# w_phi loads on SyncE's queue, a phi mask in three parts, and new orders on five engines, in a transformer layer tuned by explicit instruction lists

## Chip, cores, metric

One core of a Trainium2 chip. The metric is the device time of one execution in microseconds (us). Ratios are those of the record, of one kernel's fast runs to the other's of the same rounds, with a 95% interval; they are not quite the ratio of the medians that are quoted.

## The reference, cut

```python
x = A_x                                     # 1 x 2048 x 576, bf16
h = x + A(layernorm(x))                     # linear attention, 32 heads of 18
h2 = h + B(layernorm(h))                    # B normalizes again; 576 -> 4608 gelu -> 576
# A: q, k, v = x @ wqkv;  pq = q @ w_phi[head];  pk = k @ w_phi[head]
#    phi = [softmax(p), softmax(-p)];  kv = phi_k^T v;  z = sum phi_k
#    o = (phi_q kv) / (phi_q z + 1e-6);  return o @ wo
```

The kernel folds w_phi into the k and q weights first (it transposes wk, multiplies it with a block-diagonal phi), then walks over 16 tiles of 128 tokens.

## The kernel before

Every instruction is recorded under a label, and PLAN lists for each engine the order of the labels. Semaphore waits are derived from what each instruction reads and writes. So a label that stands early in an engine's list, and waits, holds up everything behind it on that engine. The labels that matter (t is a tile, c a block of 128 of the 576 features):

- lx, lwk, lwv, lphi: loads of x, k weights, v weights, w_phi. wq: transposing loads of q weights. B: bulk loads of MLP and output weights. T: transpose of a normalized tile by DMA (tiles 0 and 1: by TensorE).
- S: statistics of a tile, P: its rstd (the reciprocal of its standard deviation) on GpSimd, Y: its normalization. STAT and NORM say which engine does S and Y (D VectorE, A ScalarE, P GpSimd).
- A: transposes of wk and copies out of PSUM, the memory that TensorE writes to. F: folded k weights. W: folded q weights. K, V, G, Q: the products per tile for keys, values, kv and queries. R, M: VectorE's sums and scalings of a tile.

```python
STAT = "DDDADDAADADADADA"
NORM = "DDDPPPPPPPPPAPPP"
PHI = "pool"
PLAN = {
    "pe": (
        "warm0 warm2 warm3 A0 A1 warm4 A2 A3 A4 T0 F0 F1 F2 F3 F4 T1 K0 W0 W2 W3 W1 K1 V0 W4 K2 W5 V1 K3 G0 "
        # ... cut: K, V, G, Q of later tiles, attention of tiles 0 and 1
    "dve": (
        "z0 zy3 zy2 pads z2 z4 zy1 S0 z3 z1 zy0 S1 A1 Y0 Y1 A5 S2 F1 F5 F3 pads2 Y2 S4 S5 R0 M0 R1 W5 M1 R2 "
        # ... cut
    "pool": (
        "- P0 phi P1 masks P2 P3 Y3 P4 Y4 Y5 P6 Y6 Y7 P8 Y8 Y9 P10 Y10 Y11 b1c P12 P14 Y15 Y13 Y14 Ns1 L0 L1"
    "sp": (
        "lwk0 lx1 lx2 lwk2 lwk4 lwv4 lx3 wq3 wq2 wq0 wq4 wq1 lwv T2 B16 T3 B3 T4 b1 x4 B11 T5 x5 T6 T7 T8 B8 "
        "B1 B17 T9 B5 B0 T10 T11 B2 T12 B13 B12 B9 T13 T14 T15 B10 w2b0 B15 B7 B6 w2b8 B4 B14"
# ... cut
    P.at("phi")                       # one operation, waits for all three w_phi loads
    P.add(PHI, lambda e: e.tensor_tensor(
        phib[0:126, :, :].rearrange("p b (g j) -> p b g j", g=7),
        wphi_st[0:126, :, :].unsqueeze(2).to_broadcast([126, 5, 7, DH]),
        mask7[0:126, :, 0:1].unsqueeze(1).to_broadcast([126, 5, 7, DH]), ALU.mult),
        reads=WPH + [res("mask7")], writes=[res("phib")])
```

The softmax here doesn't subtract the row's maximum and nothing guards it: scores larger than these inputs give would overflow.

Of the kernel before, what the change touches and what calls it, by code (L numbers as in the profile page):

```python
# [6 lines left out]
ALU = mybir.AluOpType  # L7
# [231 lines left out]
def bass_sequential_preLN__linear_kernel_hedgehog__mixer_channel_mlp__prompt_kernel(  # L239
# [12 lines left out]
    _build(nc, A_x, A_wqkv, A_w_phi, A_wo, B_w1, B_b1, B_w2, B_b2, out)  # L252


PAIRS = [(0,), (1,), (2,), (3,)] + [(t, t + 1) for t in range(4, 16, 2)]
STAT = "DDDADDAADADADADA"
NORM = "DDDPPPPPPPPPAPPP"
TURN = "EEDDDDDDDDDDDDDD"
TCOPY = "AADD"
ACOPY = "ADAAAD"  # L260
WARM = "0111"
FCOPY = "ADADAD"
WCOPY = "AAAAAD"
PHI = "pool"
PLAN = {
    "pe": (
        "warm0 warm2 warm3 A0 A1 warm4 A2 A3 A4 T0 F0 F1 F2 F3 F4 T1 K0 W0 W2 W3 W1 K1 V0 W4 K2 W5 V1 K3 G0 "
        "Q0 V2 G1 K4 V3 G2 K5 Q1 G3 V4 Q2 K6 G4 V5 Q3 K7 V6 Q4 K8 G5 V7 G6 K9 G7 Q5 V8 K10 Q6 G8 V9 K11 Q7 "
        "V10 K12 G9 Q8 V11 G10 K13 G11 V12 K14 Q9 V13 G12 K15 Q10 V14 G13 V15 Q18 Q11 G14 G15 Q19 N0 N1 Q20 "
        "Q12 Q13 Q14 O0 Q15 L0 O1 Q16 L1 Q17 Q21 U0 Q22 U1 Q23"  # L270
    ).split(),
    "act": (
        "lx0 lphi2 lphi0 lphi1 exp A0 S3 A2 A4 A3 T0 F0 F2 F4 T1 K0 W0 W1 K1 S6 K2 W2 W3 W4 K3 S7 Q0 K4 S9 K5 "
        "Q1 S11 Q2 K6 Q3 K7 S13 Q4 K8 K9 Q5 S15 K10 Y12 Q6 K11 Q7 K12 Q8 K13 K14 Q9 K15 Q10 Q11 Q18 Q19 Q20 "
        "Q12 Q13 Q14 O0 Q15 O1 Q16 Q17 Q21 U0 Q22 Q23 gelu"
    ).split(),
    "dve": (
        "z0 zy3 zy2 pads z2 z4 zy1 S0 z3 z1 zy0 S1 A1 Y0 Y1 A5 S2 F1 F5 F3 pads2 Y2 S4 S5 R0 M0 R1 W5 M1 R2 "
        "M2 R3 M3 R4 S8 M4 R5 M5 R6 S10 M6 R7 M7 R8 S12 M8 S14 R9 M9 R10 M10 R11 M11 R12 M12 R13 M13 R14 R15 "
        "M14 M15 kvr Nc0 Ns0 Nc1 Ni0 Nm0 Ni1 Nm1 L0 L1 U1"  # L280
    ).split(),
    "pool": (
        "- P0 phi P1 masks P2 P3 Y3 P4 Y4 Y5 P6 Y6 Y7 P8 Y8 Y9 P10 Y10 Y11 b1c P12 P14 Y15 Y13 Y14 Ns1 L0 L1"
    ).split(),
    "sp": (
        "lwk0 lx1 lx2 lwk2 lwk4 lwv4 lx3 wq3 wq2 wq0 wq4 wq1 lwv T2 B16 T3 B3 T4 b1 x4 B11 T5 x5 T6 T7 T8 B8 "
        "B1 B17 T9 B5 B0 T10 T11 B2 T12 B13 B12 B9 T13 T14 T15 B10 w2b0 B15 B7 B6 w2b8 B4 B14"
    ).split(),
}

# [1 line left out]
def _build(nc, A_x, A_wqkv, A_w_phi, A_wo, B_w1, B_b1, B_w2, B_b2, out):  # L292
    S = 2048
    D = 576
    H = 32
    DH = 18
# [13 lines left out]
    P = Prog(nc)  # L310
# [34 lines left out]
    wkst = w2a[:, 0:6, :].rearrange("p m d -> p (m d)")[:, 0:3200].rearrange("p (c k) -> p c k", c=5)  # L345
    w2b = RB[:, 0:NW2B * D].rearrange("p (m d) -> p m d", m=NW2B)

    mask7 = sb("mask7", [128, 7, 19])
# [4 lines left out]
    mask25 = OTR[:, 0:475].rearrange("p (h d) -> p h d", h=25)  # L353
    wphi_st = OTR[:, 480:570].rearrange("p (b j) -> p b j", b=5)
    phib = OTR[:, 576:1206].rearrange("p (b j) -> p b j", b=5)
    oT = [OTR[:, 640 * i:640 * i + 640].rearrange("p (c t) -> p c t", c=5) for i in range(2)]
    bns = sb("bns", [128, 12], F32)
    kvr = sb("kvr", [128, 2, H, 20])
# [20 lines left out]
    bank = [Bank() for _ in range(8)]  # L379
# [3 lines left out]
    def res(name):  # L383
        if name not in R:
            R[name] = Res(name)
        return R[name]

    def rr(fmt, n):
# [7 lines left out]
          reads=[res("ident")], writes=[res("ident")])  # L396
# [3 lines left out]
          reads=[res("maskf")], writes=[res("maskf")])  # L400
    P.add("pool", lambda e: e.affine_select(maskf[:, :, :], maskf[:, :, :], pattern=[[18, 7], [0, 19]],
                                            compare_op=ALU.is_ge, fill=0.0, base=17, channel_multiplier=-1),
          reads=[res("maskf")], writes=[res("maskf")])
    P.add("pool", lambda e: e.tensor_copy(mask7[:, :, :], maskf[:, :, :]),
          reads=[res("maskf"), res("tmpo")], writes=[res("mask7")])

    WPH = rr("wphi{}", 3)
# [3 lines left out]
    P.add("dve", lambda e: e.memset(wkst[64:128, 4, :], 0.0), writes=[res("wkst4b")])  # L411
    P.add("dve", lambda e: e.memset(wkst[:, 0:4, D:D + 2], 0.0), writes=[res("wkstpad")])
    P.add("dve", lambda e: e.memset(wkst[0:64, 4, D:D + 2], 0.0), writes=[res("wkstpad")])
    P.at("z2")
    P.add("dve", lambda e: e.memset(wphi_st[:, 3, :], 0.0), writes=[res("wphi1")])
    P.at("z3")
    P.add("dve", lambda e: e.memset(wkT[:, :, 576:640], 0.0), writes=[res("wkTpad")])
    for i in range(NYB):
# [13 lines left out]
    def load(q, dst, src, writes, reads=()):  # L432
        ch = P.chan(f"ld{nch[0]}", q)
        nch[0] += 1
        P.dma(ch, lambda e: e.dma_start(dst, src), reads=reads, writes=writes)
# [15 lines left out]
    for n, (dst, src, w) in enumerate((  # L451
            (wphi_st[0:126, 0:3, :], A_w_phi[0:21].rearrange("(b h) i j -> (h i) b j", b=3), "wphi0"),
            (wphi_st[0:72, 3, :], A_w_phi[21:25].rearrange("h i j -> (h i) j"), "wphi1"),
            (wphi_st[0:126, 4, :], A_w_phi[25:32].rearrange("h i j -> (h i) j"), "wphi2"))):
        P.at(f"lphi{n}")
        load("act", dst, src, [res(w)])
    P.at("exp")
    P.add("act", lambda e: e.activation(st2[:, 0, 0:1], neghalf[:, 0:1], AF.Exp), reads=[res("neghalf")],
          writes=[res("s2_0"), res("table")])
    for c in (0, 2):  # L460
        P.at(f"lwk{c}")
        load("sp", wkst[:, c:c + 2, 0:D], A_wqkv[128 * c:128 * c + 256, D:2 * D].rearrange("(c p) m -> p c m", p=128),
             [res(f"wkst{c}"), res(f"wkst{c + 1}")])
    P.at("lwk4")
    load("sp", wkst[0:64, 4, 0:D], A_wqkv[512:576, D:2 * D], [res("wkst4")])
    P.at("lx1")
# [32 lines left out]
    def ln1_rstd(ts):  # L499
        P.at(f"P{ts[0]}")  # L500
        t0, n = ts[0], len(ts)
        st = lambda k: st1[:, k, t0:t0 + n]
        sq = [t for t in ts if STAT[t] == "A"]
        if sq:
# [10 lines left out]
        for t in ts:  # L515
            if NORM[t] == "A":
                P.add("pool", lambda e, t=t: e.tensor_scalar(st1[:, 3, t:t + 1], st1[:, 6, t:t + 1], st1[:, 5, t:t + 1],
# [59 lines left out]
    def stats(t):  # L577
        (ln1_stats_act if STAT[t] == "A" else ln1_stats_dve)(t)
        for g in PAIRS:
            if t == g[-1]:  # L580
                ln1_rstd(g)

    def lnorm(t):
        if NORM[t] != "A":
            ln1_norm({"D": "dve", "P": "pool"}[NORM[t]], t)
            return
# [7 lines left out]
    def turn_y(t):  # L594
        if TURN[t] == "E":
            ln1_petr(t, 512 * 6, {"A": "act", "D": "dve"}[TCOPY[t]])
        else:
# [20 lines left out]
    for c in range(5):  # L618
        P.at(f"A{c}")
        if c < 4:  # L620
            for b in range(5):
                turn_mm(c, b, 512 * c + 128 * b if b < 4 else 2048 + 128 * c)
            ps_copy(ACOPY[c], wkT[0:126, 0:4, 128 * c:128 * c + 128],
                    ps_all[0:126, 512 * c:512 * c + 512].rearrange("p (b k) -> p b k", b=4),
                    [bank[c]], [res(f"wkT{c}")])
            P.at(f"warm{c + 1}")
            warm(int(WARM[c]))
        else:
            for b in range(5):
                turn_mm(c, b, 2560 + 64 * b)  # L630
            ps_copy(ACOPY[4], wkT[0:126, :, 512:576], ps_all[0:126, 2560:2880].rearrange("p (b k) -> p b k", b=5),
                    [bank[5]], [res("wkT4")])
    P.at("A5")
    ps_copy(ACOPY[5], wkT[0:126, 4, 0:512], ps_all[0:126, 2048:2560], [bank[4]], [res("wkTb")])
    turn_y(0)

    P.at("phi")
    P.add(PHI, lambda e: e.tensor_tensor(
        phib[0:126, :, :].rearrange("p b (g j) -> p b g j", g=7),
        wphi_st[0:126, :, :].unsqueeze(2).to_broadcast([126, 5, 7, DH]),  # L640
        mask7[0:126, :, 0:1].unsqueeze(1).to_broadcast([126, 5, 7, DH]), ALU.mult),
        reads=WPH + [res("mask7")], writes=[res("phib")])
    stats(1)
    P.at("pads")
    P.add("dve", lambda e: e.memset(wv[64:128, 4, :], 0.0), writes=[res("wvpad")])
# [7 lines left out]
    for g in range(4):  # L653
        n = 7 if g < 3 else 4
        P.add("pool", lambda e, g=g, n=n: e.tensor_copy(mask25[:, 7 * g:7 * g + n, :], mask7[:, 0:n, :]),
              reads=[res("mask7")], writes=[res("mask25")])
    P.add("pool", lambda e: e.tensor_copy(
        kvr[:, :, 0:25, 19:20], mask25[:, :, 0:1].unsqueeze(1).to_broadcast([128, 2, 25, 1])),
        reads=[res("mask25")], writes=[res("kvr1")])
    P.add("pool", lambda e: e.tensor_copy(  # L660
        kvr[:, :, 25:32, 19:20], mask7[:, :, 0:1].unsqueeze(1).to_broadcast([128, 2, 7, 1])),
        reads=[res("mask7")], writes=[res("kvr1")])

    def weff_mm(wT, reads, c, b, lo, hi, col):
        gs = DH * HG[b][1]
        P.add("pe", lambda e: e.matmul(ps_all[:, col:col + hi - lo], wT[0:gs, b, 128 * c:128 * c + 128],  # L666
                                       phib[0:gs, b, lo:hi], start=True, stop=True),
              reads=reads + [res("phib")], banks=[bank[col // 512]])

    def weff_main(wT, reads, c, bk):  # L670
        for b in range(4):
# [6 lines left out]
    for c in range(5):  # L678
# [3 lines left out]
        weff_tail(wkT, rd, c, 5)  # L682
        ps_copy(FCOPY[c], weffk[:, c, 0:512], ps_all[:, 512 * c:512 * c + 512], [bank[c]], [res(f"weffk{c}")])
    P.at("F5")
    ps_copy(FCOPY[5], weffk[:, :, 512:576], ps_all[:, 2560:2880].rearrange("p (c f) -> p c f", c=5),
            [bank[5]], [res("weffkb")])
# [122 lines left out]
    def weffq_units():  # L809
# [8 lines left out]
        for c in range(5):  # L818
            weff_tail(wqT, rd, c, 5)
        ps_copy(WCOPY[5], weffq[:, :, 512:576], ps_all[:, 2560:2880].rearrange("p (c f) -> p c f", c=5),  # L820
                [bank[5]], [res("weffqb")])
# [110 lines left out]
    def attn_oT(t, bset=None):  # L932
        P.at(f"O{t}")
        ob = t % 2
        rd = [res(f"obuf{ob}"), res(f"opad{ob}")]
        wr = [res(f"oT{ob}")] + (WPH + [res("phib"), res("mask25")] if t < 2 else [])
        if bset is None:
            dma_tr(oT[ob], obuf[ob][:, :], rd, wr)
        else:
            pe_tr(obuf[ob], oT[ob], 512 * bset[2], rd, wr, dup=True)  # L940
# [101 lines left out]
    while bulk:  # L1042
# [6 lines left out]
        reads=[res("mask25")], writes=[res("kvra")], banks=[bank[5], bank[6]])  # L1049
# [3 lines left out]
        reads=[res("mask7")], writes=[res("kvrb")], banks=[bank[7]])  # L1053
# [4 lines left out]
    for m0 in range(0, NW2B, 8):  # L1058
# [5 lines left out]
    S1, S2 = (6, 7, 5), (1, 2, 0)  # L1064
# [24 lines left out]
          reads=[res("neghalf")] + rr("Eq{}", NR), writes=[res("sums0")])  # L1089
# [118 lines left out]
    for r in range(NR):  # L1208
        a, b = RT * (r + 1), RT * (r + 1) + 1
# [49 lines left out]
```

## Time and profile before

| | us |
|---|---|
| time, median of the first 3 runs | 412.71 (412.15 to 413.18) |
| span of the profiled execution | 409.6 |
| first phi-weight product (F0) starts | 11.17 |
| first MLP product starts | 96.5 |
| from there to the end | 313.05 |

The page of the kernel before: busy time per engine, then TensorE's granted clock (the share of the full clock that its throttle lets through) in tenths over 40 slices of 10.2 us.

```profile
span 409.6 us, 11671 instructions
...
PE 398.2 (97%) x5001; PEld 289.3 (71%) x5001; DVE 180.4 (44%) x451; ACT 180.6 (44%) x418; POOL 97.7 (24%) x130
...
PEclk9899999999999999999999999999999999999999
```

TensorE is the limit, and in the MLP, three quarters of the span, it hardly waits. The change leaves that part's code alone. So all that can be had is in the first 96.5 us. The chain of waits of the kernel before, 5 to 17 us (start, us, what), shows the prologue:

```profile
2.33 3.73 DMA OTR<-in_A_w_phi_dram
6.06 1.72 issue
7.78 1.30 POOL OTR L638
9.08 0.20 POOL st L511
...
9.35 0.58 POOL st L513
...
10.04 0.43 DVE ybuf L526
10.47 0.61 DVE RA L604
...
11.17 1.50 PE ps_all L666 x30
12.67 0.42 PE ps_all L563 x5
13.09 2.42 PE ps_all L744 x10
```

L638 is the phi mask, L511 and L513 tile 1's rstd, L526 its normalization, L604 the copy A5, L666 the F products, L744 a K group. The 1.72 us called issue are GpSimd's wait for the last of the three w_phi loads, which landed at 7.65 us. The rstd stands behind the mask in GpSimd's list although it does not need it. K0 takes 2.42 us, at half clock, later K groups 1.23 us. TensorE's waits in the first 100 us (us in total, times, longest):

```profile
PE ps_all L666 <- DVE RA L604: 2.6, 1, 2.6
PE ps_all L744 <- DMA yT<-ybuf: 1.4, 2, 1.1
...
```

The second line is the K groups waiting for a tile transposed by DMA (yT).

### The profile page before, as it was taken

Reading aid. Unit: us, or ns where it says so; the run is one execution under the profiler, and the core shown is the slowest. Engines: PE = TensorE matmul, PEld = TensorE weight load, DVE = VectorE, ACT = ScalarE, POOL = GpSimd, SP = SyncE. Lnnn points to the kernel's source line nnn. Section 1 sums busy time; section 2 is a strip of 40 time slices with the busy share of each in tenths; the row PEclk is TensorE's granted clock in tenths of the full one; section 3 lists DMA queues with packets and bytes.
Section 4 is the critical chain, followed back from the end, with each engine's and each line's share of the span. In section 5 each row is a group of like instructions: output and inputs, shape, how many; then the busy total and the mean of one; then the engine's idle time right before and its main releaser. Section 6 shows DMA issues by size and latency. Waiting matters only on the chain.

```text
span 409.6 us, 11671 instructions
## 1 busy us (share of the span) xinstructions
PE 398.2 (97%) x5001; PEld 289.3 (71%) x5001; DVE 180.4 (44%) x451; ACT 180.6 (44%) x418; POOL 97.7 (24%) x130
## 2 busy tenths in 40 slices
PE   5999999999999999999999999999999999999996
PEld 2566666858965796589559956985697579658953
DVE  4898998886445125422443234234324412300000
ACT  5686764568850274037205710660075026404700
POOL 4868680012202202210320022002200220111000
PEclk9899999999999999999999999999999999999999
DMA  9875974292211100111120111111100110000000
GB/s 231 187 173 103 256 190 99 67 387 99 35 25 41 32 18 18 32 33 20 27 30 23 19 34 30 29 24 32 32 18 19 30 32 19 18 14 19 2 2 29
DMA packets 45596, 25.87 MB, mean 63 GB/s; under 512 B 32745, under 2 KB 44521, under 8 KB 45545
## 3 DMA queue, kind: packets, MB, share of 16 engines
q1 hardware_dynamic: 44784, 24.97, 24.8%
q8 instruction: 39, 0.64, 0.6%
q10 hardware_dynamic: 760, 0.17, 0.3%
q14 instruction: 13, 0.10, 0.1%
HBM read 15.13 MB, written 2.36 MB: 43 GB/s over the span
## 4 chain that ended last, share of the span: by engine, by line
PE 87%; DVE 5%; DMA 3%; POOL 2%; issue 1%; ACT 1%; ACTq 0%; DVEq 0%; POOLq 0%
PE ps_all L1125 35%; PE ps_all L1193 35%; PE ps_all L950 5%; PE ps_all L744 4%; PE ps_all L761 3%; PE ps_all L829 2%; DMA yT<-ybuf 2%; PE ps_all L850 2%; PE ps_all L799 1%; POOL ybuf L526 1%; DMA OTR<-in_A_w_phi_dram 1%; DVE x_all L970 1%; ACT RB L751 1%; PE ps_all L666 0%; DVE RB L784 0%
## 5 line engine op out<-in xcount | busy, mean ns | idle before, releaser
L1136 ACT ACTIVATE RA<-ps_all,b1T 128x256 bf16<-128x256 f32 x288 | 115.0, 479 | 176.7 <-PE ps_all L1125 162.1
L1125 PE MATMUL ps_all<-yT,w1sb 64*128 64x256 bf16 x2304 | 151.9, 269 | 0.0
L1125 PEld LDWEIGHTS ps_all<-yT,w1sb 64*128 64x128 bf16 x2304 | 136.2, 94 | 5.1
L1193 PE MATMUL ps_all<-w2a,RA 128*128 128x512 bf16 (+1 forms) x640 | 96.2, 286 | 0.0
L1193 PEld LDWEIGHTS ps_all<-w2a,RA 128*128 128x128 bf16 x640 | 45.8, 98 | 35.6 <-ACT RA L1136 1.5
L1125 PE MATMUL ps_all<-yT,w1t 64*128 64x256 bf16 x288 | 70.8, 270 | 0.0
L1193 PE MATMUL ps_all<-RB,RA 128*128 128x64 bf16 (+1 forms) x512 | 67.7, 286 | 0.0
L1202 DVE TENSOR_TENSOR WQ<-ps_all,tmpo 128x64 bf16<-128x64 f32 (+1 forms) x32 | 14.7, 458 | 101.2 <-PE ps_all L1193 88.9
L1193 PEld LDWEIGHTS ps_all<-RB,RA 128*128 128x128 bf16 x512 | 33.5, 98 | 32.3
L970 DVE SCALAR_TENSOR_TENSOR x_all<-ps_all,x_all 128x576 bf16<-128x576 f32 x16 | 12.1, 758 | 82.4 <-PE ps_all L950 82.4
L982 POOL TENSOR_TENSOR st<-st,neghalf 128x1 f32<-128x1 f32 x16 | 8.8, 552 | 134.6 <-DVE st L984 134.6
L918 POOL TENSOR_TENSOR obuf<-tpn 128x576 bf16<-128x576 f32 x14 | 19.6, 1400 | 86.5 <-DVE tpn L913 76.4
L1199 POOL TENSOR_TENSOR tmpo<-x_all,b2bc 128x576 f32<-128x576 bf16 x16 | 20.4, 1273 | 43.2 <-DVE WQ L1202 43.2
L950 PE MATMUL ps_all<-wo_sb,OTR 64*128 64x288 bf16 x288 | 29.7, 283 | 0.2
L835 ACT ACTIVATE Eq<-ps_all 128x512 bf16<-128x512 f32 (+1 forms) x48 | 25.1, 526 | 9.2 <-PE ps_all L829 8.3
L526 POOL TENSOR_SCALAR ybuf<-x_all,st 128x576 bf16<-128x576 bf16 x12 | 27.5, 2296 | 1.1 <-POOL st L513 0.9
L1125 PEld LDWEIGHTS ps_all<-yT,w1t 64*128 64x128 bf16 x288 | 26.3, 94 | 1.9
L751 ACT ACTIVATE RB<-ps_all 128x576 bf16<-128x576 f32 x32 | 19.1, 648 | 16.3 <-PE ps_all L744 13.7
L829 PE MATMUL ps_all<-yT,WQ 128*128 128x256 bf16 x200 | 25.2, 273 | 0.2 <-ACT Eq L835 0.2
L744 PE MATMUL ps_all<-RA,yT 128*128 128x512 bf16 (+1 forms) x160 | 23.4, 296 | 1.5 <-DMA yT<-ybuf 1.4
L784 DVE TENSOR_TENSOR RB<-ps_all,RB 128x1152 bf16<-128x1152 f32 x16 | 21.5, 1348 | 4.9 <-PE ps_all L761 4.7
L761 PE MATMUL ps_all<-RB,yT 128*128 128x512 bf16 (+1 forms) x160 | 22.2, 286 | 0.0
(104 smaller groups left out, 313.5 us busy)
## 6 DMA issues: line engine op xcount, KB each, us to landing
w1sb<-in_B_w_dram SPq DMA_DIRECT2D x8, 576.0 KB, 6.3
w2a<-in_B_w_dram SPq DMA_DIRECT2D x4, 720.0 KB, 7.2
RB<-in_B_w_dram SPq DMA_DIRECT2D x2, 1152.0 KB, 7.8
out_dram<-WQ SPq DMA_DIRECT2D x16, 144.0 KB, 1.8
x_all<-in_A_x_dram SPq DMA_DIRECT2D x3, 576.0 KB, 5.3
w2a<-in_A_wqkv_dram SPq DMA_DIRECT2D x2, 288.0 KB, 4.4
RB<-in_A_wqkv_dram SPq DMA_DIRECT2D x1, 576.0 KB, 4.5
w1t<-in_B_w_dram SPq DMA_DIRECT2D x2, 288.0 KB, 4.5
```

What stands on the lines that cost most here:

```text
L526: P.add(eng, lambda e: e.tensor_scalar(ybuf[yb][:, 0:D], src, mean, rstd, ALU.subtract, ALU.mult), reads=[r_src, *r_st], writes=[res(f"ybu ...
L744: P.add("pe", lambda e, c=c, o=o, n=n: e.matmul(ps_all[:, 512 * KB + o:512 * KB + o + n], yT[:, c, sl * 128:(sl + 1) * 128], weffk[:, c, o ...
L751: P.add("act", lambda e, s=s: e.activation(Ek[eb][:, D * s:D * s + D], ps_all[:, 512 * KB:512 * KB + D], AF.Exp, scale=1.0 if s == 0 else ...
L761: P.add("pe", lambda e, c=c, o=o, n=n: e.matmul(ps_all[:, 512 * VB + o:512 * VB + o + n], yT[:, c, sl * 128:(sl + 1) * 128], wv[:, c, o:o ...
L784: P.add("dve", lambda e: e.tensor_tensor(vx(t)[:, :, :, 0:DH], ps_all[:, 512 * VB:512 * VB + D].rearrange("p (h d) -> p h d", h=H).unsquee ...
L829: P.add("pe", lambda e, i=i, c=c, h0=h0: e.matmul(ps_all[:, 512 * bk + RW * i:512 * bk + RW * i + RW], weffq[:, c, DH * h0:DH * h0 + 128], ...
L835: P.add("act", lambda e, s=s: e.activation(Eq[:, r, s, bs[0]:bs[0] + n, :], ps_all[:, 512 * bk:512 * bk + RW * n].rearrange("p (b t) -> p ...
L950: P.add(lane, lambda e: e.matmul(ps_all[:, 512 * bk:512 * bk + DHF], oT[ob][h:h + 64, c, :], wo_sb[h:h + 64, c, o:o + DHF], start=first, s ...
L1125: P.add(lane, lambda e: e.matmul(ps_all[:, o:o + RW], lhs, yT[h:h + 64, c, ys], start=first, stop=not begin and i == 1 and c == 3, skip_gr ...
L1136: P.add("act", lambda e, m=m, o=o: e.activation(hmid[:, m, :], ps_all[:, o:o + RW], AF.Gelu_apprx_tanh, bias=b1T[:, m:m + 1]), reads=[res( ...
L1193: P.add("pe", lambda e, m=m, bk=bk, o=o, n=n: e.matmul(ps_all[:, 512 * bk:512 * bk + n], w2_lhs(m, j), w2_rhs(m, o, n), start=(m == 0), st ...
L1199: P.add("pool", lambda e: e.tensor_tensor(tmpo[:, :], x_all[:, t, :], b2bc[:, :], ALU.add), reads=[res("b2"), res(f"x{t}")], writes=[res(" ...
```

## The change

Its intent: take w_phi off ScalarE's queue, let parts of the mask start as parts of w_phi land, and use an order in which TensorE waits less. The diff, cut:

```diff
-STAT = "DDDADDAADADADADA"
-NORM = "DDDPPPPPPPPPAPPP"
+STAT = "DDDADDAAAADADADA"
+NORM = "DDDDPPPPPPPPPAPD"
-PHI = "pool"
+PHI = "PDP"
 PLAN = {
     "pe": (
-        "... T1 K0 W0 W2 W3 W1 K1 V0 W4 K2 W5 V1 K3 G0 "                      (cut)
+        "... T1 K0 V0 K1 W0 W1 W2 W3 K2 W5 V1 W4 K3 G0 G1 V2 "                (cut)
     "pool": (
-        "- P0 phi P1 masks P2 P3 Y3 P4 Y4 Y5 P6 Y6 Y7 P8 Y8 Y9 P10 Y10 Y11 b1c P12 P14 Y15 Y13 Y14 Ns1 L0 L1"
+        "- P0 P1 phi0 phi2 P3 P2 P4 Y4 P6 Y5 Y6 Y7 P8 Y8 masks Y9 P10 Y10 Y11 P12 Y12 P14 b1c Y14 Ns1 L0 L1"
     "sp": (
-        "lwk0 lx1 lx2 lwk2 lwk4 lwv4 lx3 wq3 wq2 wq0 wq4 wq1 lwv T2 B16 T3 B3 T4 b1 x4 B11 T5 x5 T6 T7 T8 B8 "
-        "B1 B17 T9 B5 B0 T10 T11 B2 T12 B13 B12 B9 T13 T14 T15 B10 w2b0 B15 B7 B6 w2b8 B4 B14"
+        "lx1 lx2 lwk0 lwk2 lphi0 lwk4 lphi2 lphi1 lwv4 lx3 lwv wq3 wq4 wq1 wq0 wq2 T2 T3 T4 x4 B10 T5 B8 B11 "
+        "B15 T6 x5 B2 T7 B5 T8 B3 T9 T10 T11 T13 B7 b1 T12 T15 B0 B12 T14 w2b0 B4 B9 B6 B17 w2b8 B1 B13 B14 "
+        "B16"
@@
-        load("act", dst, src, [res(w)])
+        load("sp", dst, src, [res(w)])
@@
+    for k, (b0, b1, nr) in enumerate(((0, 3, 126), (3, 4, 72), (4, 5, 126))):
+        P.at(f"phi{k}")
+        P.add({"D": "dve", "P": "pool"}[PHI[k]], ...                           (one mask per load; cut)
```

Cut besides: the new lists of ScalarE and VectorE, some copies that change engine, one warm-up matmul fewer, a memset that is no longer needed.

## The prediction

> **What bounds it now.** The page gives PE 97% busy over a 409.6 us span; by the chain of waits the MLP matmuls alone are 69%. From about 96.5 us (first MLP matmul in the timeline) the chain is PE with almost no gap, and the change leaves that code and its order alone. So only the first 96.5 us can move. There the timeline shows dead or slow PE time in these places: the prologue until 11.17 us, when the first phi-weight product (F0) starts; K0 at half clock (2.42 us against 1.23 us for each later ten-matmul group; granted clock 0.5 from 12.68 to 16.09 us, 0.77 mean in 10 to 15 us); one wait of 1.14 us at 30.05 us for a transposed tile (yT, landing 5.4 us after issue behind bulk loads); one of 0.28 us at 62.5 us; about 2 us in the attention tail (77 to 96 us), which is a latency chain that keeps its order. K and V groups in between run at 1.23 us, with no slack.
>
> **What the change does.** Before, the last of three w_phi loads landed at 7.7 us, GpSimd masked phi as one 1.30 us operation (7.78 to 9.08) and only then made tile 1's rstd (0.23 + 0.57 us); VectorE waited 2.1 us for that rstd in front of the copy (A5) that released F0. After, the rstd comes before phi; phi is 3/5 + 1/5 on GpSimd (estimate 0.78 + 0.26 us) and a small piece on VectorE. The w_phi loads now share SyncE's queue behind the first two k-weight loads (landed 7.38 us before). The Trainium skill ("DMA: Bandwidth & Descriptors", Queues, rings and completion order) says each ring is consumed in order while different queues are served in turn; so I expect w_phi to land at 8 to 9.3 us, later than before, and to become the new gate. F0 then starts near 9.4 us: 1.7 us earlier. The shorter PE pause should also avoid some of the half-clock window ("TensorE: Matmul & The Clock Gate", Part 1: about 3.4 us windows; the trace's 3.41 us record agrees).
>
> Given back: VectorE has four weight copies (about 0.65 us each) before K0 can end (near 13.0 us, before 15.5), then ScalarE puts 1.75 us of statistics in front of the K0 and K1 exponentials, so I expect K2 at about 17.7 us, 1.7 us early after counting a shifted W4. GpSimd loses two 2.29 us normalizations (tiles 3 and 15 go to VectorE at 0.43 us; 12 changes with 13), so tiles 5 to 11 are ready 3 to 7 us earlier and the 1.14 us wait goes, partly replaced by one near K3 (T3 lands about 21.5 us). VectorE's sum hardly changes (one 1.2 us statistics group less; two norms, one small mask and a copy more).
>
> **Sum.** At K5, estimate 2.0 us ahead; with the 62.5 us wait gone 2.3 us; tail and MLP unchanged. 412.7 - 2.4 = 410.3 us. Range 408.6 to 412.4. Chances: faster than 2% 0.02, within 2% 0.96, slower 0.02.
>
> **What would show it.** F0 at 9 to 10 us (not 11.2); w_phi landing later than 7.7 us; no VectorE wait for tile 1's rstd; K5 about 2 us earlier net of work done; no PE wait over 0.5 us for yT between 25 and 75 us; first MLP matmul at 94.2 us instead of 96.5; the span after it within 0.5 us of 313 us.
>
> **What would make it wrong.** w_phi landing after 10 us behind bulk traffic (prologue gain gone); PE stalls for K2/K3 tiles or the wq transposes, now issued about 2 us later; tile 12's transpose waiting behind two bias transposes and a weight load (about 52 us); VectorE, over 90% busy from 40 to 65 us, becoming the limiter; MLP weights now loaded last arriving late at 119 us.

## The result, and the profile after

| | before | after |
|---|---|---|
| time, median of 4 runs | 412.94 us (412.15 to 413.55) | 409.95 us (409.37 to 410.55) |
| ratio | | 0.9929 (0.9905 to 0.9953) |
| again, in the rounds of e12 (11 and 6 runs) | 412.35 us | 410.00 us, ratio 0.9952 (0.9932 to 0.9973) |

A gain of 2.35 to 3 us, under 1%; both intervals lie under 1. The profiled execution of after has a span of 408.5 us, only 1.1 us under that of before; the first experiment deals with that. The page of after:

```profile
span 408.5 us, 11674 instructions
...
PE 398.3 (97%) x5000; PEld 288.5 (71%) x5000; DVE 180.7 (44%) x450; ACT 182.4 (45%) x422; POOL 93.7 (23%) x129
...
PEclk9999999999999999999999999999999999999999
```

Its chain of waits, 0 to 18 us:

```profile
1.71 5.11 DMA w2a<-in_A_wqkv_dram
6.82 0.05 issue
6.86 2.67 PE ps_all L615 x25
9.54 0.53 PE ps_all L564 x5
10.07 0.03 issue
10.10 0.76 PE ps_all L668 x11
...
10.95 0.79 DVE RA L605 x2
...
12.15 1.08 DVE RA L605 x2
```

F0 (now L668) starts at 10.10 us. Neither the rstd nor the mask is in the chain any more: it runs through the k-weight load and its transposes (L615). These ran at half clock here: 25 of them took 2.67 us, against 0.72 + 0.88 us of work before. TensorE's waits in the first 100 us:

```profile
PE ps_all L615 <- DMA w2a<-in_A_wqkv_dram: 1.6, 1, 1.6
...
PE ps_all L746 <- ACT tpn L486: 1.1, 1, 1.1
...
PE ps_all L746 <- DVE RA L605: 0.5, 1, 0.5
PE ps_all L746 <- DMA yT<-ybuf: 0.5, 1, 0.5
```

The wait of 1.1 us is put down to ScalarE, but that had long been done: K6 started at 33.30 us, and tile 6's transpose had landed at 33.17 us. So K6 (1.08 us) and K7 (0.46 us) both waited for yT. The chain of after, 28 to 40 us:

```profile
30.09 7.25 DMA yT<-ybuf
37.35 0.14 issue
37.48 1.39 PE ps_all L746 x10
```

Tile 7's transpose took 7.25 us from issue to landing; the median of the 14 is 2.7 us. Just ahead of it in SyncE's queue stood a bulk weight load and a load of x, and before these tile 6's transpose with another bulk load ahead of it. The row of DMA busy share of after, 20 to 40 us in slices of 0.5 us, shows the engines nearly full from 22 us on:

```profile
DMA  1782969999999999898999948999999949899999
```

**How the traces are compared.** The TensorE orders differ, so a start time alone does not compare. For each K group I took its start and subtracted the work that this kernel's TensorE list has before it, each group at its full-clock duration in the traces (K 1.23, V 1.23, G 0.56, Q 1.09 or 0.55, W 0.24, F 0.25, A 0.29, T 0.28 us; warm-up matmuls count nothing). The rest is what TensorE has lost up to there, by waits or half clock. "MLP" is the same at the first MLP product (before it I count 80.2 us of work, the same in every kernel, so differences in a column matter and not its level). Some matmul records are missing from eight of the fourteen traces, so single entries are good to about 0.2 us. All in us:

| kernel | F0 starts | lost at K4 | K5 | K8 | K10 | K15 | MLP |
|---|---|---|---|---|---|---|---|
| before | 11.2 | 11.4 | 12.7 | 12.7 | 12.6 | 13.0 | 16.3 |
| e1 before again | 10.4 | 11.6 | 11.8 | 11.6 | 13.8 | 14.9 | 18.1 |
| after | 10.1 | 10.0 | 10.0 | 11.8 | 11.8 | 11.8 | 14.9 |
| e12 after again | 9.3 | 9.8 | 9.8 | 11.0 | 11.0 | 10.9 | 14.0 |
| e2 rstd before phi | 10.1 | 11.3 | 11.5 | 11.3 | 13.2 | 14.0 | 17.3 |
| e5 before, bulk later | 10.6 | 12.2 | 13.6 | 13.6 | 13.5 | 13.5 | 16.8 |
| e6 before, Y3 on VectorE | 11.5 | 12.1 | 13.3 | 13.2 | 13.5 | 14.0 | 17.2 |
| e9 before, rstd, wv, V0 | 10.0 | 10.7 | 11.7 | 11.5 | 11.9 | 12.4 | 15.7 |
| e10 e9 with bulk later | 10.2 | 10.7 | 10.9 | 10.6 | 12.8 | 12.8 | 16.0 |
| e3 after, w_phi on ScalarE's queue | 8.9 | 8.8 | 8.8 | 10.7 | 10.6 | 12.1 | 15.2 |
| e4 after, bulk later | 9.6 | 9.8 | 9.8 | 9.8 | 9.8 | 10.6 | 13.8 |
| e8 after, one mask | 9.7 | 9.7 | 9.7 | 10.9 | 10.9 | 10.9 | 14.0 |
| e11 after, wv late | 9.8 | 14.6 | 14.6 | 14.6 | 14.6 | 14.9 | 18.1 |
| e7 combined | 9.0 | 9.8 | 9.8 | 9.8 | 9.8 | 9.8 | 12.9 |

With two traces each, before loses 11.5 us on average up to K4 and after 9.9: 1.6 us gained in the prologue. From K4 to K15 before loses 1.6 and 3.3 us more, after 1.8 and 1.1: 1.0 us gained on average. From K15 to the MLP 0.1 to 0.2 us is gained, in the MLP 0.3 us is lost. The sum, 2.4 us, is the difference of the mean spans (410.5 and 408.1) and lies in the range of the timed gains.

The 0.3 us of the MLP (313.05 us before, 313.37 us after, in every variant of each) is one pause of TensorE, at the same matmul 275 us into it. What makes it stays open. Where the 1.0 us between K4 and K15 comes from is not shown either: queue order, earlier tiles and chance are not separated there.

### The profile page after: what moved, and what is told of

It is laid out like the page before. It is cut to its first block, busy times and chain, and to the rows that moved or that the text cites. A ratio compares the mean times of both kernels' runs of the same rounds, so it can differ in the third digit from the quotient of the medians.

```text
span 408.5 us, 11674 instructions
## 1 busy us (share of the span) xinstructions
PE 398.3 (97%) x5000; PEld 288.5 (71%) x5000; DVE 180.7 (44%) x450; ACT 182.4 (45%) x422; POOL 93.7 (23%) x129
## 4 chain that ended last, share of the span: by engine, by line
PE 87%; DMA 4%; DVE 4%; POOL 2%; ACT 1%; issue 1%; SPq 0%; DVEq 0%; POOLq 0%
PE ps_all L1127 35%; PE ps_all L1195 35%; PE ps_all L952 4%; PE ps_all L763 3%; PE ps_all L831 3%; PE ps_all L746 3%; PE ps_all L852 2%; DMA yT<-ybuf 2%; PE ps_all L801 2%; DMA w2a<-in_A_wqkv_dram 1%; DMA x_all<-in_A_x_dram 1%; PE ps_all L615 1%; DVE x_all L972 1%; POOL ybuf L527 1%; DVE RA L605 0%
## 5 line engine op out<-in xcount | busy, mean ns | idle before, releaser
L972 DVE SCALAR_TENSOR_TENSOR x_all<-ps_all,x_all 128x576 bf16<-128x576 f32 x16 | 12.1, 758 | 82.2 <-PE ps_all L952 82.1
L837 ACT ACTIVATE Eq<-ps_all 128x512 bf16<-128x512 f32 (+1 forms) x48 | 25.3, 526 | 14.6 <-PE ps_all L831 13.4
L746 PE MATMUL ps_all<-RA,yT 128*128 128x512 bf16 (+1 forms) x160 | 22.4, 286 | 2.5 <-ACT tpn L486 1.1
L527 POOL TENSOR_SCALAR ybuf<-x_all,st 128x576 bf16<-128x576 bf16 x10 | 22.9, 2296 | 0.6 <-POOL st L514 0.6
```

Of the source, the lines that this page charges most:

```text
L527: P.add(eng, lambda e: e.tensor_scalar(ybuf[yb][:, 0:D], src, mean, rstd, ALU.subtract, ALU.mult), reads=[r_src, *r_st], writes=[res(f"ybu ...
L746: P.add("pe", lambda e, c=c, o=o, n=n: e.matmul(ps_all[:, 512 * KB + o:512 * KB + o + n], yT[:, c, sl * 128:(sl + 1) * 128], weffk[:, c, o ...
L837: P.add("act", lambda e, s=s: e.activation(Eq[:, r, s, bs[0]:bs[0] + n, :], ps_all[:, 512 * bk:512 * bk + RW * n].rearrange("p (b t) -> p ...
```

## The experiments

Each was timed over 5 rounds in four-kernel batches: e1 to e4 (before: median 412.46 us), e5 to e8 (411.65), e9 to e12 (412.35). All results were correct.

**e1_before_again.** Before with a comment changed.

> The kernel before, unchanged but for a comment. Timed runs of before and after lie 2.9 us apart, the two profiled runs only 1.1 us apart. Theory A (chance: where the clock windows and DMA waits fall differs from run to run, and the profile of before was a lucky one): this profile has a span of 410 to 412 us, with more time at half clock or a longer yT wait than the first profile (F0 near 11.2 us again), and the timed runs spread over 1 us or more. Theory B (the timed gap has a steady cause that the profile hides): the span is again 409.6 us within 0.3 and the timed runs stay at 412 to 413.5.

Measured: 411.61 us (411.26 to 413.15), ratio 0.9990 (0.9965 to 1.0015); the profiled span is 411.4 us. The 11 runs of before itself lie between 410.72 and 413.57 us. TensorE's waits in this trace of the same program:

```profile
PE ps_all L744 <- DMA yT<-ybuf: 3.5, 4, 1.2
PE ps_all L666 <- ACT yT L567: 1.5, 1, 1.5
```

The yT waits are 3.5 us, not 1.4. Theory A holds in the span, the yT waits and the spread, though not in its F0 (10.42 us, not near 11.2): the first profile of before was a lucky one, and one profile of each kernel cannot carry a difference of 1 us. Part of the scatter is the clock: full from 5.9 us with a half-clock stretch at 12.7 to 16.1 us in the first trace, half at 10.6 to 14.0 us in this one, none after 5.8 us in e2's, half in that of after until 10.3 us, where its record of full clock begins (its matmuls before that took twice the time). The Trainium skill ("TensorE: Matmul & The Clock Gate", Part 1) says that the clock is decided in free-running windows of 3413 ns, so that the same kernel meets it differently from run to run. The records agree: the two half-clock stretches are 3.41 us long each. The clock alone does not order the times, though: one run of before took 412.94 us at a mean clock of 1.0, another 410.80 us at 0.996.

The mean clocks settle a rival: that after gains only because it meets fewer half-clock windows. One such window takes 0.4% off a run's mean clock (0.996 in this trace, which has one). In the rounds of e1 to e12, 21 of 33 runs of before have a mean clock of 0.996 or less, of the ten runs of after one. But at equal clock the gain is still there: in the rounds of e12 the four runs of before at 0.999 or more average 412.2 us, the five such runs of after 410.0 us. (The mean leaves out what came before the first clock record, so it does not count after's half clock until 10.3 us.)

**e2_rstd_before_phi.** Before with

```diff
-        "- P0 phi P1 masks
+        "- P0 P1 phi masks
```

> Before, with one exchange on GpSimd: tile 1's rstd ahead of the phi mask. If the gate of F0 was that rstd standing behind phi (my theory), F0 starts at 9.2 to 9.6 us instead of 11.2, and 1.2 to 1.9 us of it reach the end: ratio 0.995 to 0.997. If the later waits for yT absorb it, or the w_phi landing itself was the gate, the ratio is 0.999 or more and F0 moves by under 0.5 us.

Measured: 411.69 us, ratio 0.9993 (0.9964 to 1.0022). F0 came at 10.09 us, about 1 us early and later than I expected, and at K4 nothing of it was left (11.3 us lost). The trace shows where it went:

```profile
PE ps_all L761 <- DMA RB<-in_A_wqkv_dram: 1.1, 1, 1.1
```

L761 is V0. It now waited for the v weights, which SyncE issues behind five transposing loads of 1.2 to 1.3 us issue time each, and which landed at 17.17 us. So my main reason was only the first of two gates.

**e3_phi_on_act_queue.** After with the three w_phi loads back on ScalarE's queue, masks still in three parts.

```diff
-        load("sp", dst, src, [res(w)])
+        load("act", dst, src, [res(w)])
```

> After, with the three w_phi loads back on the ScalarE queue (masks in three parts kept). In the trace of after F0 waited for the weight copy behind the third k load (7.98 us) and not for phi, so moving them back should change little: F0 within 0.5 us of 10.1, ratio to after 0.998 to 1.002 (to before 0.991 to 0.995). The rival, that the queue move is what pays, expects F0 at 11 us and 1 us or more lost (ratio to before over 0.995).

Measured: 409.53 us, ratio 0.9944 (0.9918 to 0.9970): the time of after. w_phi landed at 6.5 us instead of 9.0, F0 came at 8.9 us, and 1 us was gained up to K4. It was given back at later yT waits (K6, K7 and K12; lost at K15: 12.1 us, after 11.8). The Trainium skill ("DMA: Bandwidth & Descriptors", Issuing engines are not separate DMA queues) says that a second issuing engine saves only issue time. That fits: the last w_phi load took 4.6 us from issue to landing on SyncE's queue (issued at 4.47 us), about 4.2 on ScalarE's (issued at 2.32 us), and landed early because it was issued early. So the move in the title is not what pays.

**e4_bulk_later.** After with four bulk loads (B15, B2, B5, B3; my text below says three) behind later transposes.

```diff
-        "B15 T6 x5 B2 T7 B5 T8 B3 T9 T10 T11 T13 B7 b1 T12
+        "T6 x5 T7 T8 B15 B2 T9 T10 B5 T11 B3 T13 B7 b1 T12
```

> After, with three bulk weight loads (w2a, two w1sb) put behind later tile transposes in SyncE's order. If the two waits of after (1.08 us before K6, 0.46 us before K7, transposes landing 7 us after issue) come from bulk loads ahead in the same queue, both fall under 0.3 us and 1.0 to 1.5 us are gained: ratio to before 0.988 to 0.991. If the transposes are slow for another reason (GpSimd's tiles late, x5), the waits stay and the time is that of after.

Measured: 409.15 us (408.02 to 409.56), ratio 0.9928 (0.9904 to 0.9951), a smaller gain than expected. The loss at K6 and K7 went from 1.8 us to nothing (9.8 at K5, 9.8 at K8), so the bulk loads ahead in the queue are the cause of those waits. What is left of waits for yT is one, at K12, whose transpose stands behind a bulk load and the two bias transposes; 0.9 us came back there.

```profile
PE ps_all L746 <- DMA yT<-ybuf: 0.7, 1, 0.7
```

By time, e4 is not separated from after (0.9929 and 0.9952, in other rounds).

**e5_before_bulk_later.** Before with T9 to T15 ahead of bulk loads.

```diff
-        "... T7 T8 B8 B1 B17 T9 B5 B0 T10 T11 B2 T12 B13 B12 B9 T13 T14 T15 B10 w2b0 ...
+        "... T7 T8 T9 B8 B1 B17 T10 T11 B5 B0 T12 T13 T14 T15 B2 B13 B12 B9 B10 w2b0 ...
```

> Before, with the bulk weight loads put behind tile transposes 9 to 15 in SyncE's order, nothing else. In three traces of before and its near copy TensorE loses 0.4 to 3.4 us between K5 and K15 waiting for transposed tiles. If bulk loads ahead in SyncE's queue make these waits and the scatter of the runs, the loss from K6 to K12 falls under 0.5 us, only the wait before K13 (tile 13 normalized late on GpSimd) stays, and the time falls by 0.5 to 1.5 us: ratio 0.996 to 0.999. If GpSimd is the limiter, waits and time stay as they are (ratio 0.999 to 1.001).

Measured: 410.42 us, ratio 0.9971 (0.9947 to 0.9995). From K5 on nothing is lost any more (13.6 to 13.5 us), at K13 neither, and about 0.3% is gained with one list changed. This fits the same cause in the kernel before, but shows it less well than e4: the first trace of before lost only 0.4 us there, and this trace is of e5's slowest run (411.81 us). Up to K5 this trace lost more than that of before (13.6 against 12.7 us); T5 still stands behind the bias transposes and two loads in this list.

**e6_before_y3_on_vector.** Before with tile 3 normalized on VectorE. The diff, condensed:

```diff
-NORM = "DDDPPP...       pool: P2 P3 Y3 P4       dve: Y2 S4 S5 R0
+NORM = "DDDDPP...       pool: P2 P3 P4          dve: Y2 S4 S5 Y3 R0
```

> Before, with tile 3's normalization on VectorE instead of GpSimd (one part of the relief that the change gives GpSimd). If late tiles from GpSimd cause the waits of before, tiles 4 to 11 come 2 us earlier and 0.5 to 1.5 us are gained: ratio 0.996 to 0.999. If the queue is the limiter the ratio is 0.999 to 1.001, with the waits at the same K groups.

Measured: 411.94 us, ratio 0.9993 (0.9963 to 1.0023). K5 still loses 1.2 us, K10 0.3, K13 0.5. This part of GpSimd's relief shows no gain. But the run doesn't test what I meant it to: the tiles did not come earlier. Tiles 4, 5 and 6 were normalized by 21.6, 23.9 and 31.4 us, against 20.7, 22.9 and 30.7 in before. In after tile 6's transpose was issued at 26.54 us, against 30.69 in before. What earlier tiles are worth stays open.

**e7_combined.** After with e3's queue, e4's bulk order, and T12, T15, T14 ahead of the bias transposes. The diff, condensed:

```diff
-        "B15 T6 x5 B2 T7 B5 T8 B3 T9 T10 T11 T13 B7 b1 T12 T15 B0 B12 T14 w2b0
+        "T6 x5 T7 T8 B15 B2 T9 T10 B5 T11 T13 T12 T15 T14 B3 b1 B7 B0 B12 w2b0
-        P12 Y12 P14 b1c Y14                (pool)
+        P12 Y12 P14 Y14 b1c
```

> After, with w_phi back on ScalarE's queue (gained 1 us until K4 in its trace), bulk loads behind the transposes, and tiles 12, 14 and 15 transposed ahead of the two bias transposes. If the three add, TensorE's lost time is 9 us at K5 and under 9.7 us at K15 (after: 10.0 and 11.8), the span is 405.5 to 406.5 us and the ratio to before 0.985 to 0.989. If one of them only moves the wait to the next limiter, it is that of the bulk-later kernel alone: 0.991 to 0.994.

Measured: 408.50 us (408.11 to 409.50), ratio 0.9924 (0.9902 to 0.9946), profiled span 406.5 us. From K2 to K15 TensorE loses nothing (9.9 and 9.8 us). But the early w_phi did not help: 8.3 us lost at K1 became 9.9 at K2, because W0 now waited for the last q-weight transpose. This wait in the trace:

```profile
PE ps_all L668 <- issue: 1.5, 1, 1.5
```

(L668 also serves the W groups; the transposing load landed at 16.69 us, W0 started at 16.89.) So the three did not simply add: the ratio is the one I expected if a wait only moves on (0.991 to 0.994), not 0.985 to 0.989. It has the lowest median of all kernels, but its interval overlaps with that of after, and the two were not in the same rounds, so by time alone it is not separated from after.

**e8_phi_one_mask.** After with the mask in one piece on GpSimd. The diff, cut (left out: phi1 and phi2 leave their lists, the one mask waits for all three loads, and the memset z2 comes back):

```diff
-    for k, (b0, b1, nr) in enumerate(((0, 3, 126), (3, 4, 72), (4, 5, 126))):
+    for k, (b0, b1, nr) in enumerate(((0, 5, 126),)):
```

> After, with the phi mask in one piece again on GpSimd, at the place of the first of the three. It can start when the last w_phi load has landed (9.0 us in the trace of after) and takes 1.30 us, so F0 moves from 10.1 to about 10.4 us. If the three parts matter that is 0.3 us more lost at K2 and at most 0.3 us more time (ratio to before 0.993 to 0.995); if the split is what made F0 early, F0 is at 11 us and 1 us is lost.

Measured: 410.27 us, ratio 0.9962 (0.9937 to 0.9986). F0 came at 9.66 us, between the two traces of after (10.10 and 9.26), and 9.7 us were lost at K4. The trace shows no cost of the single mask. The interval of the time overlaps with both of after's.

**e9_rstd_and_wv.** Before with e2's exchange, wv ahead of the q transposes, and V0 ahead of the W groups. The diff, condensed:

```diff
-        lx3 wq3 wq2 wq0 wq4 wq1 lwv T2      (sp)    T1 K0 W0 W2 W3 W1 K1 V0 W4 K2 W5 V1 K3   (pe)
+        lx3 lwv wq3 wq2 wq0 wq4 wq1 T2              T1 K0 V0 K1 W0 W2 W3 W1 K2 W4 W5 V1 K3
-        T1 K0 W0 W1 K1 S6 K2                (act)
+        T1 K0 K1 W0 W1 S6 K2
```

> Before, with three things together: tile 1's rstd ahead of phi, the wv load ahead of the five wq transposes on SyncE, and V0 ahead of the W groups on TensorE. The rstd exchange alone made F0 1 us early, but V0 then waited 1.1 us for wv and nothing was left at K4. If wv behind the transposes is that second gate, TensorE's lost time at K4 falls from 11.3 to 12.2 us (before and its variants) to 9.8 to 10.6 us (as after), the later waits stay, and the ratio is 0.995 to 0.998. If the prologue gain of after needs the moved w_phi loads or the split mask, K4 stays above 11 us and the ratio at 0.999 or more.

Measured: 410.81 us (409.93 to 411.30), ratio 0.9962 (0.9947 to 0.9977). Lost at K4: 10.7 us, just over my bound of 10.6 but 0.6 to 1.5 us under every trace of before, e2, e5 and e6. V0 started at 13.29 us (18.07 in before) and no wait of it is left in the trace. So the gain here needs neither the w_phi move nor the split, and by time e9 is not separated from after in the same rounds (0.9952). Which of its three parts are needed was not run: wv and V0 without the rstd exchange is missing.

**e10_before_rebuilt.** e9 with

```diff
-        T4 b1 x4 B11 T5 x5 T6 T7 T8 B8 B1 B17 T9 B5 B0 T10 T11 B2 T12 B13 B12 B9 T13 T14 T15 B10
+        T4 x4 T5 x5 T6 T7 T8 T9 B11 B8 b1 B1 B17 T10 T11 B5 B0 T12 T13 T14 T15 B2 B13 B12 B9 B10
```

> The same as the run with rstd, wv and V0 exchanged, and besides the bulk loads and the bias transposes behind the tile transposes (T5 behind x4 alone). No w_phi move, no split mask, no change of who makes statistics and norms. If queue order and one exchange are the whole gain of the change, TensorE has lost 9.8 to 11 us at K15 (after: 11.8; before: 13.0 to 14.9) and the ratio is 0.990 to 0.995, that of after. If GpSimd's relief or the split is needed as well, a wait of 1 us or more at K5 to K13 is left and the ratio is over 0.996.

Measured: 411.65 us, ratio 0.9984 (0.9960 to 1.0008), profiled span 409.3 us. My bound for K15 was missed (12.8 us), and the time with it. The loss at K5 fell to 0.2 us, but at K10 one wait of 2.0 us came:

```profile
50.78 1.39 PE L744 MATMUL ps_all<-RA,yT 128*128 128x512 bf16 x10 [2.04 <-DMA yT<-ybuf]
```

Tile 10 was ready at about 45.0 us; SyncE was then still issuing the loads and bias transposes that I had put between T9 and T10, issued T10 at 46.41 us behind a 576 KB and a 144 KB load, and it landed at 50.65 us. The time has a second side: e10's three runs at a mean clock of 0.998 or more took 410.28 to 411.07 us, about as e9, and the three at 0.995 to 0.996 took 412.23 to 412.79. The profiled run is one of the fast three, so this trace does not show what slowed the others. So this run does not settle whether order alone gives the whole gain; it shows once more that a load in the wrong place undoes it.

**e11_after_wv_late.** After with wv behind the q transposes.

```diff
-        lx3 lwv wq3 wq4 wq1 wq0 wq2 T2
+        lx3 wq3 wq4 wq1 wq0 wq2 lwv T2
```

> After, with the wv load behind the five wq transposes again, nothing else. If wv's place is needed for the prologue gain, V0 (13.7 us in after) waits for wv until about 15.5 us, the lost time at K4 rises from 10.0 to 11 us or more, and 1 to 1.8 us are lost: ratio to before 0.995 to 0.998. If not, it stays as after, 0.991 to 0.995.

Measured: 413.94 us (413.40 to 414.51), ratio 1.0039 (1.0023 to 1.0054): slower than before, 3.9 us slower than after in the same rounds. The direction is as expected, the size more than twice it:

```profile
PE ps_all L763 <- DMA RB<-in_A_wqkv_dram: 3.3, 1, 3.3
```

V0 in after, and then in e11:

```profile
13.71 1.39 PE L763 MATMUL ps_all<-RB,yT 128*128 128x512 bf16 x10
17.04 2.56 PE L763 MATMUL ps_all<-RB,yT 128*128 128x512 bf16 x10 [3.34 <-DMA RB<-in_A_wqkv_dram]
```

wv landed at 16.90 us, not at the 15.5 that I expected, and in after V0 stands ahead of K1, so the wait stops K1 as well. Behind the wait the trace has a half-clock stretch, 17.05 to 20.46 us: V0 took 2.56 us instead of 1.39, K1 1.90 instead of 1.40. All six runs have a mean clock of 0.996 or less. So the loss is the wait and about 1.7 us of half clock. wv's place and V0's place belong together.

**e12_after_again.** After with a comment changed.

> After, unchanged but for a comment, to have its scatter, a second trace and a ratio from the same rounds as the others: ratio to before 0.991 to 0.995, lost time at K15 of 11 to 12.5 us with waits before K6 and K7 of 0.3 to 1.5 us each; if the gain over before in the first measurement was luck, the ratio is over 0.996.

Measured: 410.00 us (409.44 to 412.20), ratio 0.9952 (0.9932 to 0.9973), profiled span 407.7 us, K6 and K7 losing 1.2 us together (1.8 in the first trace); lost at K15: 10.9 us, 0.1 under my bound. The gain was no luck, and the yT waits of after come again.

## Why the prediction was right, point by point

- **The time.** 410.3 us predicted, 409.95 and 410.00 measured: inside the range of 408.6 to 412.4. The gain predicted was 2.4 us; measured 3.0 and 2.35.
- **Where.** "Only the first 96.5 us can move": right; the MLP changed by 0.3 us. The first MLP product was predicted at 94.2 us and came at 95.2 and 94.3.
- **The prologue.** No wait of VectorE for tile 1's rstd is left (2.1 us in before), as predicted. F0 predicted near 9.4 us, measured 10.10 and 9.26; K2 at 17.7, measured 17.9 and 18.0. "At K5, estimate 2.0 us ahead": by lost time 1.8 to 2.9 us over the four pairs of traces. The size was right, the reason incomplete. I gave the rstd behind the mask as the cause. Moving it alone (e2) brought F0 1 us forward and nothing to K4; the v weights were the second gate, and I did not name them. e9 adds their move and V0's and reaches 10.7 us at K4; e11 takes the weights' move away from after and loses 4.6 to 4.8 us there, half clock included. So that the size came out was partly luck: gains that I had not counted (wv, V0) stood in for one that would not have come alone.
- **w_phi.** Predicted to land at 8 to 9.3 us "and to become the new gate". It landed at 8.4 to 9.0 us in the two traces of after. The number fits, the reason that I gave (in-order rings, the section of the Trainium skill that the prediction names) is not what the runs show: by e3 it lands later because it is issued later, 4.47 us against 2.32. Nor was it the gate in the first trace of after: there TensorE was busy with the k-weight and tile transposes at half clock until 10.07 us and started F0 at 10.10 without a wait. The split mask and the queue move show no gain (e8, e3).
- **The clock.** I expected the shorter pause to avoid some of the half-clock time. Such windows are rarer in after (see e1), but they are not what makes the gain.
- **yT waits.** "No PE wait over 0.5 us for yT between 25 and 75 us" was wrong: 1.08 us before K6. I credited GpSimd's earlier tiles and overlooked that the new SyncE order puts bulk loads ahead of T6 and T7. e4 shows that the queue order makes these waits; e6 was meant to test earlier tiles, but did not make them earlier. The wait near K3 that I expected did not come: T3 landed at 20.66 us, K3 started at 20.85. Of the risks listed, the bias transposes ahead of tile 12 were real (e3: 1.5 us at K12, e4: 0.9).
- **Scatter.** I took one trace of before as the kernel. Another of the same program has 1.8 us more lost at the MLP.

What is shown: wv's place is needed in after (e11), and with the rstd exchange and V0's place it gives more than half of the gain by time in before, by the ratios without their intervals (e9, 0.9962 against 0.9929 and 0.9952); the place of bulk loads relative to tile transposes makes later waits in after (e4) and in a rebuilt before (e10), and by e5 probably in before. What stays open: whether the rstd exchange is needed beside wv and V0, how much the changes of statistics, norms and copies add, and the exact share of each part, since most are under the scatter of 1 us.

## What to carry to other kernels

A queue that carries both bulk loads and small transfers that the next step waits for should be ordered by when each is needed; bulk can stand behind the small ones as long as its own deadline is far, but e10 shows that moving it needs care: put in front of another small transfer it makes a new wait. When a gate is removed and the time does not move, look at what the same engine waits for next before giving up the idea: here the first gate removed alone (e2) paid nothing, and both together (e9) did; the second alone was not run. For differences under 1%, take two traces of the same program before explaining one.

## What the Trainium skill lacked or had wrong

- "DMA: Bandwidth & Descriptors" says that a ring is consumed in order, but gives no figure for what that costs a small transfer: a tile transpose of one and the same size took 2.6 us from issue to landing alone and 7.25 us behind bulk loads (both in after).
- The same page treats back-pressure only for remote DMA. Here some issues themselves became longer while bulk loads were under way on the same queue (that these are the cause was not tested): a tile transpose held SyncE for 2.31 us instead of 1.20 (after), a 144 KB load for 2.34 instead of 0.43 us (e1), and all later issues with it.
- The same page has no issue time of a transposing DMA measured on trn2 (its passage on trn3 lists sequencer cycles for "previous generations", small tiles): here mostly 1.20 to 1.30 us of SyncE each, against 0.4 to 0.6 us for most plain loads.
- "TensorE: Matmul & The Clock Gate" is right about the free-running window (3.41 us in both half-clock records); how much of a 400 us kernel's run-to-run scatter (410.3 to 413.6 us for before) comes from it no page says, beyond putting the warm-up penalty under 1% of a typical span. Here the 12 runs of before at a mean clock of 0.999 or more average 411.9 us, the 18 at 0.994 to 0.996 412.0 and the three at 0.991 to 0.992 413.0; the chips are mixed, so this only says that one window explains little.
